# An attention and FFN kernel: RMS weight loaded first, GpSimd's order pinned, two more FFN tiles on the first token half

## The chip, the cores and the metric

The kernel runs on one core of one Trainium2 chip. The metric is device microseconds (us) of one execution, the median of several. The kernel before takes 265.59 us (median of 3, 265.25 to 265.94). Every execution also has a mean granted TensorE clock, as a share of full rate.

## The reference

Windowed attention with four sink tokens, then a SwiGLU FFN with an RMS norm in front. Cut to what matters:

```python
# q, k, v: (4, 8, 768, 64); keep = is_sink (first 4 keys) | (0 <= row - col < 128)
scores = np.where(keep, scale * q @ k^T, -1e9)
x = softmax(scores) @ v                # -> (3072, 512) tokens x channels
xn = x / sqrt(mean(x * x) + 1e-6) * rms_g
g = xn @ w_gate                        # 512 -> 1536
out = (g * sigmoid(g) * (xn @ w_val)) @ w_out
```

## The kernel before

The 3072 tokens are 24 blocks of 128. Four blocks form a group G of 512 tokens for the FFN. TensorE alternates pieces of attention ("slots") with pieces of the FFN ("parts"); the function `weave` decides the order. GpSimd issues the q, k, v and weight loads, one after the other; the sync engine (SP) issues the rest.

The order of GpSimd's loads in the opening, in program order (a scheduler may move a load where the order isn't pinned):

```python
load_q(0); load_k(0); load_q(1); load_k(1); load_v(0); load_v(1); load_w(0)
load_q(2); load_k(2); load_w(1); load_q(3); load_v(2); load_k(3); load_v(3)
load_w(2); load_w(3); load_q(4); load_w(4); load_k(4); load_w(5)   # w: 256 of 1536 columns, gate and val
load_v(4)
for g in range(GB + 1, 2 * GB):            # GB = 4
    load_q(g); load_k(g); load_v(g)
load_wo(0); load_wo(1)                     # output weights, 1.5 MB
for g in range(2 * GB, NB): ...            # blocks 8 to 23
```

The opening and the first group. The first two blocks are done alone; the gate and value products of group 0 then run on the first token half (blocks 0 and 1, 256 columns), for FFN tiles 0 to FA - 1, while blocks 2 and 3 are still in attention. The second half and the other tiles follow:

```python
unit_warm(6)                               # six idle matmuls, 2.74 us
... # blocks 0 and 1
nc.vector.tensor_copy(out=gb[:, 0:1], in_=QKT[0][:, 1, 0, 0:1])   # holds the next load back
load_gb()                                  # RMS weight, broadcast to 128 partitions, 256 KB, from SP
...
unit_x(1)                                  # transposes of the normed x of block 1
unit_t1(2, 1)                              # transposes of block 2's k
...
fa, fb = [], []
for ft in range(0, FA, 2):                 # FA = 8
    fa += parts_f(0, (ft, ft + 1), slice(0, GN // 2))     # [gate, val], first token half
    fb += parts_f(0, (ft, ft + 1), slice(GN // 2, GN))    # second token half
for ft in range(FA, FTN):                  # FTN = 12
    fb += parts_f(0, (ft,), slice(0, GN))
weave(fa, [..., [lambda: unit_x(2), ...], [lambda: unit_x(3)]], first=True)
slots = [[lambda: unit_t1(4, 1), lambda: unit_t1(5, 0)],          # block 5's q transposes
         [lambda: unit_s(4, 0), lambda: unit_t1(5, 1)],           # scores need block 5's q
         [lambda: unit_s(4, 1)], [lambda: unit_sink_scores(0, 4)], [lambda: unit_t(6)], []]
```

The softmax here doesn't subtract the row's maximum and nothing guards it: scores larger than these inputs give would overflow.

Of the kernel before, what the change touches and what calls it, by code (L numbers as in the profile page):

```python
# [9 lines left out]
ALU = mybir.AluOpType  # L10
ACT = mybir.ActivationFunctionType
FP32 = mybir.dt.float32
BF16 = mybir.dt.bfloat16
I32 = mybir.dt.int32

P = 128
# [12 lines left out]
def kernel(  # L29
# [13 lines left out]
    nc = tc.nc  # L43

    B, H, S, D = q.shape
    DM = H * D
    DFF = moe_w_gate.shape[1]
    NS = int(n_sink)
# [14 lines left out]
    NEG = -32768.0  # L63
# [2 lines left out]
    DMA_T_FROM = 12  # L66

    DMA_X_FROM = 8
    FA = 8
    WEAVE_FROM = 9  # L70
    POOL_MASK_FROM = 2
    MANUAL = {mybir.EngineType.PE, mybir.EngineType.SP}
# [8 lines left out]
    xpool = ctx.enter_context(tc.tile_pool(name="xpool", bufs=3))  # L81
# [17 lines left out]
    gb = const.tile([P, DM], FP32, name="gb")  # L99
# [16 lines left out]
    def load_q(g):  # L116
        QS[g] = load_block(q, "qs", g)

    def load_k(g):
        KS_[g] = load_block(k, "ks", g)  # L120

    def load_v(g):
        b, t = divmod(g, NT)
        nc.gpsimd.dma_start(
            out=V16[b][:, t, :, 0:D],
            in_=v[b, :, t * P:(t + 1) * P, :].rearrange("h t d -> t h d"),
        )
# [7 lines left out]
    def load_w(c):  # L135
        cols = slice(c * WCH, (c + 1) * WCH)
        nc.gpsimd.dma_start(out=wg[:, :, cols], in_=wg_src[:, :, cols])
        nc.gpsimd.dma_start(out=wv[:, :, cols], in_=wv_src[:, :, cols])

    def load_wo(c):  # L140
# [4 lines left out]
    ident = const.tile([P, P], BF16, name="ident")  # L145
# [4 lines left out]
    amasks = const.tile([P, 2, 2, P], BF16, name="amasks")  # L150
# [3 lines left out]
    sel = const.tile([P, P], BF16, name="sel")  # L154
    nc.vector.memset(sel, 0.0)
    headm = const.tile([P, H], BF16, name="headm")
    nc.vector.memset(headm, 1.0)

    load_q(0)
    load_k(0)  # L160
    nc.gpsimd.affine_select(
        out=ident, in_=ident, compare_op=ALU.not_equal, fill=1.0,
        base=0, pattern=[[-1, P]], channel_multiplier=1,
    )
    load_q(1)
    nc.gpsimd.affine_select(
        out=amasks[:, 1, 0, :], in_=amasks[:, 1, 0, :], compare_op=ALU.is_ge,
        fill=NEG, base=0, pattern=[[1, P]], channel_multiplier=-1,
    )
    nc.vector.tensor_scalar(  # L170
        out=amasks[:, 1, 1, :], in0=amasks[:, 1, 0, :], scalar1=-1.0, scalar2=NEG,
        op0=ALU.mult, op1=ALU.add,
    )
    nc.vector.tensor_copy(out=amasks[:, 0, :, :], in_=amasks[:, 1, :, :])
    nc.vector.memset(amasks[0:NS, 0, :, :], 0.0)
    load_k(1)
    load_v(0)
    load_v(1)
    load_w(0)
    load_q(2)  # L180
    load_k(2)
    load_w(1)
    load_q(3)
    load_v(2)
    load_k(3)
    load_v(3)
    nc.gpsimd.affine_select(
        out=sel[:, 0:H * NS].rearrange("p (h s) -> p h s", s=NS),
        in_=sel[:, 0:H * NS].rearrange("p (h s) -> p h s", s=NS),
        compare_op=ALU.not_equal, fill=1.0,  # L190
        base=0, pattern=[[0, H], [-1, NS]], channel_multiplier=1,
    )
    nc.gpsimd.affine_select(
        out=headm, in_=headm, compare_op=ALU.is_ge, fill=0.0,
        base=0, pattern=[[-NS, H]], channel_multiplier=1,
    )
    nc.gpsimd.affine_select(
        out=headm, in_=headm, compare_op=ALU.is_ge, fill=0.0,
        base=NS - 1, pattern=[[NS, H]], channel_multiplier=-1,
    )  # L200
    load_w(2)
    load_w(3)
    load_q(4)
    load_w(4)
    load_k(4)
    load_w(5)
    load_v(4)
    for g in range(GB + 1, 2 * GB):
        load_q(g)
# [19 lines left out]
    def unit_t1(g, i):  # L229

        b, t = divmod(g, NT)
        if t == 0 and i == 0:
            QKT[b] = qkt.tile([P, 2, HP, S], BF16, name="qkT")
        kind = dict(tag="ph", bufs=6) if PROLOGUE[0] and g == 2 else dict(tag="b1")
        ps = pp[0].tile([P, 512], FP32, name="pqk", **kind).bitcast(BF16)
        transposes(ps, (QS, KS_)[i].pop(g), 0)
        (nc.scalar.copy if g != 1 and i == 0 else nc.vector.tensor_copy)(  # L237
            out=QKT[b][:, i, :, t * P:(t + 1) * P],
            in_=ps[:, 0:HP * P].rearrange("p (x c) -> p x c", c=P),
        )  # L240

    def load_gb():
        nc.sync.dma_start(
            out=gb, in_=moe_rms_g.rearrange("(o d) -> o d", o=1).to_broadcast((P, DM)),
        )

    def by_dma(g):
# [222 lines left out]
    def unit_rms(g):  # L470
# [31 lines left out]
        if g >= 2:  # L502
            unit_xr(g)
# [3 lines left out]
    def unit_xr(g):  # L507
        y, x16 = Y.pop(g), X16.pop(g)
        XR[g] = []
        for c in halves(g):  # L510
            XR[g].append(xpool.tile([P, c.stop - c.start], BF16, name="xr", bufs=4))
            nc.vector.scalar_tensor_tensor(  # L512
                out=XR[g][-1], in0=x16[:, c], scalar=y[:, 4:5], in1=gb[:, c],
                op0=ALU.mult, op1=ALU.mult,
            )
        if g >= DMA_X_FROM:
            G, tb = divmod(g, GB)
            if tb == 0:
                XNT[G] = xtpool.tile([P, KTN, GN], BF16, name="xnt")
            nc.sync.dma_start_transpose(  # L520
                out=XNT[G][:, :, tb * P:(tb + 1) * P], in_=XR.pop(g)[0],
            )
# [120 lines left out]
    with tc.manual_schedule(engines=MANUAL_ALL):  # L643
        unit_warm(6)
        unit_t1(0, 0)
        unit_bias(0, 0)
        unit_t1(0, 1)
        unit_bias(0, 1)
        unit_sp(0, 0)
        unit_t1(1, 0)  # L650
        unit_bias(1, 0)
        nc.vector.tensor_copy(out=gb[:, 0:1], in_=QKT[0][:, 1, 0, 0:1])
        load_gb()
        unit_sp(0, 1)
        unit_t1(1, 1)
        unit_av(0, 0)
        unit_norm(0, 0, PV[(0, 0)])
        unit_sp(1, 0)
        unit_av(0, 1)
        unit_norm(0, 1, PV[(0, 1)])  # L660
        unit_sq(0, 0)
        unit_sq(0, 1)
        unit_warm(WARM[0])
        for u in range(2):
            unit_av(1, u)
            unit_norm(1, u, PV[(1, u)])
            unit_sq(1, u)
        unit_rms(0)
        unit_xr(0)
        unit_rms(1)  # L670
        unit_xr(1)
        unit_warm(WARM[1])
        unit_x(0)
        unit_t1(2, 0)
        unit_warm(WARM[2])
        unit_x(1)
        unit_t1(2, 1)
        nc.vector.tensor_scalar(
            out=masks, in0=amasks, scalar1=-1.0 / NEG, scalar2=1.0,
            op0=ALU.mult, op1=ALU.add,  # L680
        )
        pools.close()
        pp[0] = ctx.enter_context(
            tc.tile_pool(name="psum", bufs=4, space=bass.MemoryType.PSUM)
        )
        PROLOGUE[0] = False

    with tc.manual_schedule(engines=MANUAL):


        fa, fb = [], []
        for ft in range(0, FA, 2):
            fa += parts_f(0, (ft, ft + 1), slice(0, GN // 2))
            fb += parts_f(0, (ft, ft + 1), slice(GN // 2, GN))
        for ft in range(FA, FTN):
            fb += parts_f(0, (ft,), slice(0, GN))
        weave(fa, [
            [lambda: unit_bias(1, 1), lambda: unit_sp(1, 1), lambda: unit_sink(0)],
            [lambda: unit_t1(3, 0), lambda: unit_s(2, 0)],
            [lambda: unit_s(2, 1), lambda: unit_sink_scores(0, 2)],  # L700
            [lambda: unit_t1(3, 1), lambda: unit_bias(3, 0), lambda: unit_av(2, 0), lambda: unit_sp(3, 0), lambda: unit_av(2, 1)],
            [lambda: unit_av(3, 0)],
            [lambda: unit_av(3, 1), lambda: unit_t1(4, 0)],
            [lambda: unit_x(2), lambda: unit_bias(3, 1), lambda: unit_sp(3, 1)],
            [lambda: unit_x(3)],
        ], first=True)
        slots = [[lambda: unit_t1(4, 1), lambda: unit_t1(5, 0)], [lambda: unit_s(4, 0), lambda: unit_t1(5, 1)], [lambda: unit_s(4, 1)], [lambda: unit_sink_scores(0, 4)], [lambda: unit_t(6)], []]
        for g in range(5, NB + 3):
            slots += step(g)
        slots[6].pop()  # L710
        slots[10].pop()
        outs = []
        n = 0
        for G in range(NG):

            parts = fb if G == 0 else []
            for ft in range(FTN if G > 0 else 0):
                parts += parts_f(G, (ft,), slice(0, GN))
                if ft % 3 == 2 and outs:
                    parts += outs.pop(0)  # L720
            outs = [parts_o(G, tb) for tb in range(GB)]
            if G < WEAVE_FROM or G == NG - 1:
                for o in outs:
                    parts = parts + o
                outs = []
            n1 = 6 + 4 * ((G + 2) * GB + 2 - 5) + 1
            weave(parts, slots[n:n1], 1)
            n = n1
# [33 lines left out]
```

## Time and profile before

| | before |
|---|---|
| time | 265.59 us |
| span of the profiled execution | 263.1 us |
| TensorE busy | 94% |
| TensorE busy, first 50 us | 39.7 of 50 us |
| output products of group 0 begin | 61.71 us |

First the page: the line of busy times, and the slices (40 of 6.6 us each; a digit is tenths busy, or tenths of full clock granted). TensorE is full nearly everywhere but in the opening, and its clock drops in the third and fourth slice.

```profile
PE 246.1 (94%) x1746; PEld 123.6 (47%) x1746; DVE 179.9 (68%) x472; ACT 138.2 (53%) x277; POOL 98.2 (37%) x131
...
PE   5867979999999999999999998999999999999994
...
PEclk9988999999999999999999999999999999999999
```

The chain of work that ended last, followed back from the last instruction; columns are start, duration and what. Between 11 and 38.7 us it is a chain of loads, and its last link is block 5's q.

```profile
11.25 9.23 DMA wv<-in_moe_w_val_dram
...
21.15 8.07 DMA wv<-in_moe_w_val_dram
...
29.50 9.18 DMA qs<-in_q_dram
...
39.13 0.89 PE pg L552 x8
```

The timeline of TensorE: start, duration, what, and in brackets the idle time before it and what ended it. `pw` are idle warm-up matmuls, `pxt` the x transposes, `pqk` the q and k transposes, `pg` and `pvl` gate and value products, `pT` and `pss` the scores, `po` the output products.

```profile
12.46 1.89 PE L313 MATMUL pw<-idle 128*128 128x512 bf16 x8
16.90 0.40 PE L534 MATMUL pxt<-ident,xr 128*128 128x128 bf16 x4 [2.55 <-DVE xr L512]
...
17.36 2.00 PE L313 MATMUL pw<-idle 128*128 128x512 bf16 x5
...
35.38 0.40 PE L534 MATMUL pxt<-ident,xr 128*128 128x128 bf16 x4 [1.21 <-DVE xr L512]
...
38.73 0.40 PE L224 MATMUL pqk<-ident,qs 128*128 128x128 bf16 x4 [0.37 <-DMA qs<-in_q_dram]
38.96 1.04 PE L552 MATMUL pg<-xnt,wg 128*128 128x256 bf16 x8
39.93 0.39 PE L367 MATMUL pT<-qkT 64*128 64x256 bf16 x4
...
61.71 1.03 PE L593 MATMUL po<-wo,hT 128*128 128x512 bf16 x4
```

Five warm-up matmuls take 2.00 us after the 2.55 us gap, eight took 1.89 us before it. The record of the clock has half rate from 17.69 to 21.10 us. The 2.55 us gap is a wait for VectorE, and VectorE waited for the RMS weight (timeline of VectorE):

```profile
16.09 0.75 DVE L512 SCALAR_TENSOR_TENSOR xr<-x_342,y,gb 128x512 bf16<-128x512 bf16 x1 [1.52 <-DMA gb<-in_moe_rms_g_dram]
```

### The profile page before, as it was taken

The numbers are of one execution on the slowest core, as the hardware profiler recorded it, in microseconds if no ns is written. First come the engines' busy times: TensorE is split into PE (matmuls) and PEld (weight loads), VectorE is DVE, ScalarE is ACT, GpSimd is POOL, SyncE is SP. The second block draws the span as 40 slices with busy tenths as digits, with TensorE's granted clock in tenths as the row PEclk, the third lists the DMA queues.
The fourth block names the chain that finished last, engine by engine and source line by source line (L and its number), as shares of the span: only waits on it lengthen the run. The fifth ranks groups of instructions, "written<-read, shape, count | busy, mean of one in ns | idle before, by whom it ended". The sixth has DMA issues, their size and how long they took to land.

```text
span 263.1 us, 4755 instructions
## 1 busy us (share of the span) xinstructions
PE 246.1 (94%) x1746; PEld 123.6 (47%) x1746; DVE 179.9 (68%) x472; ACT 138.2 (53%) x277; POOL 98.2 (37%) x131
## 2 busy tenths in 40 slices
PE   5867979999999999999999998999999999999994
PEld 1435757645454444444454443444444454444441
DVE  3653786899768999438898449799338894078700
ACT  2635667687886546456455454465554532233211
POOL 8978679389989260413212001114212000000000
PEclk9988999999999999999999999999999999999999
DMA  9999999999999999452111450312330112200022
GB/s 58 138 176 178 186 169 174 197 156 151 169 178 174 146 143 147 95 159 42 22 21 40 97 165 20 62 20 41 102 101 1 22 20 60 107 16 0 0 80 80
DMA packets 105990, 25.73 MB, mean 98 GB/s; under 512 B 95088, under 2 KB 102768, under 8 KB 105968
## 3 DMA queue, kind: packets, MB, share of 16 engines
q0 software_dynamic: 82784, 14.16, 75.6%
q1 hardware_dynamic: 23184, 11.28, 18.6%
q8 instruction: 13, 0.21, 0.4%
q14 instruction: 9, 0.07, 0.1%
HBM read 28.57 MB, written 6.29 MB: 133 GB/s over the span
## 4 chain that ended last, share of the span: by engine, by line
PE 73%; DMA 10%; DVE 6%; ACT 4%; POOL 3%; issue 2%; ACTq 0%; POOLq 0%
PE pg L552 22%; PE po L593 21%; PE pvl L552 21%; DMA wv<-in_moe_w_val_dram 7%; PE pT L367 4%; DMA qs<-in_q_dram 3%; ACT et L374 2%; PE pv L427 1%; PE pv L423 1%; DVE et L387 1%; PE pqk L224 1%; PE pss L299 1%; PE pv L415 1%; DVE xr L512 1%; POOL qs L111 1%
## 5 line engine op out<-in xcount | busy, mean ns | idle before, releaser
L552 PE MATMUL pg<-xnt,wg 128*128 128x512 bf16 (+1 forms) x320 | 74.3, 359 | 2.3 <-DVE p_2576 L570 1.7
L552 PE MATMUL pvl<-xnt,wv 128*128 128x512 bf16 (+1 forms) x320 | 74.0, 358 | 0.2 <-ACT xnt L538 0.2
L593 PE MATMUL po<-wo,hT 128*128 128x512 bf16 x288 | 66.7, 379 | 0.0
L565 ACT ACTIVATE th<-pg 128x512 bf16<-128x512 f32 x72 | 42.8, 594 | 39.5 <-PE pg L552 39.1
L374 ACT ACTIVATE et<-pT 128x1024 bf16<-128x1024 f32 (+1 forms) x42 | 39.3, 936 | 10.4 <-PE pT L367 10.4
L389 POOL TENSOR_SCALAR_AFFINE_SELECT et<-et 128x512 bf16<-128x512 bf16 x20 | 12.7, 635 | 85.4 <-ACT et L374 79.6
L552 PEld LDWEIGHTS <-wg 128*128 128x128 bf16 x320 | 28.9, 98 | 29.6 <-issue 4.7
L552 PEld LDWEIGHTS <-wv 128*128 128x128 bf16 x320 | 29.6, 98 | 27.1 <-issue 1.3
L593 PEld LDWEIGHTS <-hT 128*128 128x128 bf16 x288 | 26.4, 98 | 29.5 <-issue 1.5
L600 ACT ACTIVATE osb<-po 128x512 f32<-128x512 f32 x24 | 14.3, 595 | 28.3 <-PE po L593 24.3
L111 POOL DMA_DIRECT2D qs<-in_q_dram x24 | 21.5, 897 | 7.1 <-DMA wo<-in_moe_w_out_dram 1.9
L111 POOL DMA_DIRECT2D ks<-in_k_dram x24 | 21.4, 890 | 6.5 <-DMA wo<-in_moe_w_out_dram 2.9
L450 DVE RECIPROCAL rden<-pv 128x4 f32<-128x4 f32 x48 | 8.5, 177 | 20.1 <-PE pv L427 20.0
L387 DVE TENSOR_TENSOR et<-et,masks 128x1024 bf16<-128x1024 bf16 (+1 forms) x22 | 14.1, 640 | 5.4 <-ACT et L374 5.3
L367 PE MATMUL pT<-qkT 64*128 64x256 bf16 (+1 forms) x168 | 15.6, 264 | 1.4 <-ACT qkT L237 0.7
L367 PEld LDWEIGHTS <-qkT 64*128 64x128 bf16 x168 | 5.1, 94 | 17.7 <-issue 17.5
L427 PEld LDWEIGHTS <-et 128*128 128x128 bf16 x168 | 11.6, 97 | 2.3 <-issue 0.7
L423 PEld LDWEIGHTS <-et 128*128 128x128 bf16 x136 | 10.8, 98 | 3.2
L394 POOL TENSOR_SCALAR_AFFINE_SELECT et<-et 128x512 bf16<-128x512 bf16 x16 | 11.0, 690 | 0.0
L415 PE MATMUL pv<-vsk,esk 128*128 128x260 bf16 x32 | 8.8, 274 | 0.0
L313 PE MATMUL pw<-idle 128*128 128x512 bf16 x22 | 7.4, 488 | 1.3 <-DVE idle L102 1.3
L264 ACT COPY qkT<-pqk 128x1024 bf16<-128x1024 bf16 x8 | 8.1, 1008 | 1.0 <-PE pqk L224 1.0
(319 smaller groups left out, 341.7 us busy)
## 6 DMA issues: line engine op xcount, KB each, us to landing
out_dram<-osb SPq DMA_DIRECT2D x24, 256.0 KB, 2.2
qs<-in_q_dram POOLq DMA_DIRECT2D x24, 128.0 KB, 8.2
ks<-in_k_dram POOLq DMA_DIRECT2D x24, 128.0 KB, 7.8
wg<-in_moe_w_gate_dram POOLq DMA_DIRECT2D x6, 256.0 KB, 8.5
wv<-in_moe_w_val_dram POOLq DMA_DIRECT2D x6, 256.0 KB, 8.7
wo<-in_moe_w_out_dram POOLq DMA_DIRECT2D x2, 768.0 KB, 10.5
v_100<-in_v_dram POOLq DMA_DIRECT2D x6, 128.0 KB, 8.3
v_102<-in_v_dram POOLq DMA_DIRECT2D x6, 128.0 KB, 7.7
```

Of the source, the lines that this page charges most:

```text
L111: nc.gpsimd.dma_start(out=tl, in_=src[b, :, t * P:(t + 1) * P, :].rearrange("h t d -> t h d"),)
L367: nc.tensor.matmul(out=pT[:, hi, j * 256:j * 256 + w], lhsT=QKT[b][pr, 1, hp, t * P:(t + 1) * P], rhs=QKT[b][pr, 0, hp, t * P:t * P + w], ...
L374: nc.scalar.activation(out=et[:, :, 0:nq, :].rearrange("p x n c -> p x (n c)"), in_=pT.rearrange("p i (j c) -> p (i j) c", c=256)[:, :, 0: ...
L387: nc.vector.tensor_tensor(out=ev, in0=ev, in1=mv, op=ALU.mult)
L389: nc.gpsimd.affine_select(out=et[:, :, 0, :], in_=et[:, :, 0, :], compare_op=ALU.is_ge, fill=0.0, base=0, pattern=[[0, 4], [1, P]], channe ...
L415: nc.tensor.matmul(out=pv[:, 0:HW], lhsT=ESK[(b, t)], rhs=VSK[b][:, 4 * u:4 * u + 4, :], start=True, stop=False, skip_group_check=True,)
L423: nc.tensor.matmul(out=dest, lhsT=E[(g - 1, h, 1)], rhs=V16[b][:, t - 1, h, :], start=(t == 1), stop=False, skip_group_check=True,)
L427: nc.tensor.matmul(out=dest, lhsT=E[(g, h, 0)], rhs=V16[b][:, t, h, :], start=(t == 0), stop=True, skip_group_check=True,)
L552: nc.tensor.matmul(out=ps[:, i * n:(i + 1) * n], lhsT=w_sb[:, kt, ft * P:(ft + 1) * P], rhs=XNT[G][:, kt, cols], start=(kt == 0), stop=(kt ...
L565: nc.scalar.activation(out=st["th"], in_=st["pg"], func=ACT.Tanh, scale=0.5)
L593: nc.tensor.matmul(out=st["po"], lhsT=HT[(G, ft // 2)][:, ft % 2, tb * P:(tb + 1) * P], rhs=wo[:, ft, :], start=(ft == 0), stop=(ft == FTN ...
L600: nc.scalar.mul(osb, st["po"], 0.5)
```

## The change

The intent: the RMS weight is there before it is needed; block 2's k transposes come behind the first gate product; and FFN tiles 8 and 9 also run on the first token half early, so that TensorE has work until blocks 2 and 3 join. (The change was described as also having one mask with a partial identity. The diff has no such thing.) Cut to its core:

```diff
-    FA = 8
+    FA = 10
...
+    nc.sync.dma_start(out=gb, in_=moe_rms_g...to_broadcast((P, DM)))
+    with tc.manual_schedule(engines={mybir.EngineType.Pool}):
         load_q(0)
         load_k(0)
         ...                       # same program order as before, now pinned
         load_w(5)
     load_v(4)                     # outside: the scheduler puts one v load ahead of load_w(2), at 15.87 us
...
-    xr ... bufs=4
+    xr ... bufs=3
...
-        nc.vector.tensor_copy(out=gb[:, 0:1], in_=QKT[0][:, 1, 0, 0:1])
-        load_gb()
...
-        unit_t1(2, 1)             # before the first gate part
...
-            [lambda: unit_bias(1, 1), lambda: unit_sp(1, 1), lambda: unit_sink(0)],
+            [lambda: unit_t1(2, 1), lambda: unit_bias(1, 1), lambda: unit_sp(1, 1), lambda: unit_sink(0)],
...
-            [lambda: unit_x(2), lambda: unit_bias(3, 1), lambda: unit_sp(3, 1)],
+            [lambda: unit_bias(3, 1), lambda: unit_sp(3, 1)],
+            [lambda: unit_x(2)],
+            [lambda: unit_t1(4, 1)],
             [lambda: unit_x(3)],
         ], first=True)
-        slots = [[lambda: unit_t1(4, 1), lambda: unit_t1(5, 0)], ...
+        slots = [[lambda: unit_t1(5, 0)], ...
```

More of the change, by code (lines that the diff above doesn't have):

```diff
@@ L157 @@
     nc.vector.memset(headm, 1.0)
-    load_q(0)
-    load_k(0)
-    nc.gpsimd.affine_select(
-        out=ident, in_=ident, compare_op=ALU.not_equal, fill=1.0,
-        base=0, pattern=[[-1, P]], channel_multiplier=1,
-    )
-    load_q(1)
-    nc.gpsimd.affine_select(
-        out=amasks[:, 1, 0, :], in_=amasks[:, 1, 0, :], compare_op=ALU.is_ge,
-        fill=NEG, base=0, pattern=[[1, P]], channel_multiplier=-1,
-    )
-    nc.vector.tensor_scalar(
-        out=amasks[:, 1, 1, :], in0=amasks[:, 1, 0, :], scalar1=-1.0, scalar2=NEG,
-        op0=ALU.mult, op1=ALU.add,
-    )
@@ L174 @@
-    nc.vector.tensor_copy(out=amasks[:, 0, :, :], in_=amasks[:, 1, :, :])
-    nc.vector.memset(amasks[0:NS, 0, :, :], 0.0)
-    load_k(1)
-    load_v(0)
-    load_v(1)
-    load_w(0)
-    load_q(2)
-    load_k(2)
-    load_w(1)
-    load_q(3)
-    load_v(2)
-    load_k(3)
-    load_v(3)
-    nc.gpsimd.affine_select(
-        out=sel[:, 0:H * NS].rearrange("p (h s) -> p h s", s=NS),
-        in_=sel[:, 0:H * NS].rearrange("p (h s) -> p h s", s=NS),
-        compare_op=ALU.not_equal, fill=1.0,
-        base=0, pattern=[[0, H], [-1, NS]], channel_multiplier=1,
-    )
@@ L193 @@
-    nc.gpsimd.affine_select(
-        out=headm, in_=headm, compare_op=ALU.is_ge, fill=0.0,
-        base=0, pattern=[[-NS, H]], channel_multiplier=1,
-    )
-    nc.gpsimd.affine_select(
-        out=headm, in_=headm, compare_op=ALU.is_ge, fill=0.0,
-        base=NS - 1, pattern=[[NS, H]], channel_multiplier=-1,
-    )
-    load_w(2)
-    load_w(3)
-    load_q(4)
-    load_w(4)
-    load_k(4)
-    load_w(5)
+    nc.sync.dma_start(
+        out=gb, in_=moe_rms_g.rearrange("(o d) -> o d", o=1).to_broadcast((P, DM)),
+    )
@@ new lines @@
+    with tc.manual_schedule(engines={mybir.EngineType.Pool}):
+        load_q(0)
+        load_k(0)
+        nc.gpsimd.affine_select(
+            out=ident, in_=ident, compare_op=ALU.not_equal, fill=1.0,
+            base=0, pattern=[[-1, P]], channel_multiplier=1,
+        )
+        load_q(1)
+        nc.gpsimd.affine_select(
+            out=amasks[:, 1, 0, :], in_=amasks[:, 1, 0, :], compare_op=ALU.is_ge,
+            fill=NEG, base=0, pattern=[[1, P]], channel_multiplier=-1,
+        )
+        nc.vector.tensor_scalar(
+            out=amasks[:, 1, 1, :], in0=amasks[:, 1, 0, :], scalar1=-1.0, scalar2=NEG,
+            op0=ALU.mult, op1=ALU.add,
+        )
+        nc.vector.tensor_copy(out=amasks[:, 0, :, :], in_=amasks[:, 1, :, :])
+        nc.vector.memset(amasks[0:NS, 0, :, :], 0.0)
+        load_k(1)
+        load_v(0)
+        load_v(1)
+        load_w(0)
+        load_q(2)
+        load_k(2)
+        load_w(1)
+        load_q(3)
+        load_v(2)
+        load_k(3)
+        load_v(3)
+        nc.gpsimd.affine_select(
+            out=sel[:, 0:H * NS].rearrange("p (h s) -> p h s", s=NS),
+            in_=sel[:, 0:H * NS].rearrange("p (h s) -> p h s", s=NS),
+            compare_op=ALU.not_equal, fill=1.0,
+            base=0, pattern=[[0, H], [-1, NS]], channel_multiplier=1,
+        )
+        nc.gpsimd.affine_select(
+            out=headm, in_=headm, compare_op=ALU.is_ge, fill=0.0,
+            base=0, pattern=[[-NS, H]], channel_multiplier=1,
+        )
+        nc.gpsimd.affine_select(
+            out=headm, in_=headm, compare_op=ALU.is_ge, fill=0.0,
+            base=NS - 1, pattern=[[NS, H]], channel_multiplier=-1,
+        )
+        load_w(2)
+        load_w(3)
+        load_q(4)
+        load_w(4)
+        load_k(4)
+        load_w(5)
@@ L239, in unit_t1 @@
             in_=ps[:, 0:HP * P].rearrange("p (x c) -> p x c", c=P),
-        )
-    def load_gb():
-        nc.sync.dma_start(
-            out=gb, in_=moe_rms_g.rearrange("(o d) -> o d", o=1).to_broadcast((P, DM)),
         )
@@ L510, in unit_xr @@
         for c in halves(g):
-            XR[g].append(xpool.tile([P, c.stop - c.start], BF16, name="xr", bufs=4))
+            XR[g].append(xpool.tile([P, c.stop - c.start], BF16, name="xr", bufs=3))
             nc.vector.scalar_tensor_tensor(
@@ L703 @@
             [lambda: unit_av(3, 1), lambda: unit_t1(4, 0)],
-            [lambda: unit_x(2), lambda: unit_bias(3, 1), lambda: unit_sp(3, 1)],
+            [lambda: unit_bias(3, 1), lambda: unit_sp(3, 1)],
+            [lambda: unit_x(2)],
+            [lambda: unit_t1(4, 1)],
             [lambda: unit_x(3)],
         ], first=True)
-        slots = [[lambda: unit_t1(4, 1), lambda: unit_t1(5, 0)], [lambda: unit_s(4, 0), lambda: unit_t1(5, 1)], [lambda: unit_s(4, 1)], [lambda: unit_sink_scores(0, 4)], [lambda: unit_t(6)], []]
+        slots = [[lambda: unit_t1(5, 0)], [lambda: unit_s(4, 0), lambda: unit_t1(5, 1)], [lambda: unit_s(4, 1)], [lambda: unit_sink_scores(0, 4)], [lambda: unit_t(6)], []]
         for g in range(5, NB + 3):
```

## The prediction

> **What bounds the kernel now.** TensorE is busy 94% of the 263.1 us span (page, part 1), and nearly without a gap from 60 us to the last matmuls (windows view). So the change is worth what it takes from the opening's idle time: 10.3 us in the first 50. Gaps in the TensorE timeline: 2.55 us before block 0's x transposes (16.90), 0.61 before the first gate group (20.82), 0.67 (24.85), 0.35 (29.52), 1.21 before block 2's x transposes (35.38), 0.21 before block 3's (37.74), 0.37 before block 5's q transposes (38.73). The first is the RMS weight: issued at 8.79, 7.2 us to landing; VectorE waited 1.52 us for it (xr, 16.09). The chain of waits runs through DMA: weight loads, then block 5's q, issued 29.50, 9.18 us on its way; only from 39.1 on it is mostly TensorE.
>
> **What the change does.**
> 1. Weight broadcast first on the sync queue: takes the 1.5 us wait away, and moves its 256 KB from the crowded stretch 12 to 16 us to one where the DMA engines only start. At the 170 to 180 GB/s moved there, I estimate later loads come about 1 us earlier. Block 0's q may lose 0.3 us to it.
> 2. Five warm-up matmuls take 2.00 us after the 2.55 us gap, eight took 1.89 before it. [...] the slow stretch in the trace (about 17.4 to 20.8) agrees. A 1 us gap should shorten it: up to 0.8 us.
> 3. Block 2's k transposes (0.40) move behind the first gate: the 0.61 gap goes.
> 4. Tiles 8 and 9 run their first token half early: two groups of eight 256-column matmuls, 0.87 us each by their starts, so 1.74 us of work moves ahead of block 5's wait and fills the 1.21 and 0.21 gaps. Sixteen more matmuls, but eight of 256 columns cost the same 0.87 as four of 512: no net work.
> 5. GpSimd's order is pinned; one v load comes before weight chunks 2 to 5, which costs them about the 1 us gained in step 1.
> 6. Three xr buffers for four: nothing. The diff changes no mask or identity.
>
> **The sum.** Gaps removed: 1.5 + 0.8 + 0.6 + 1.2 + 0.2 = 4.3 us. Not all counts: TensorE would reach block 5's q at about 36 us and wait there, I estimate 1.5 us. So the gain is the 1.74 us of work done before that landing, plus about 1 us by which it comes earlier: 2.7. VectorE (84 to 91% busy from 40 to 60 us) with slightly denser attention slots may take back 0.2. From 60 us on the same work is only shifted; the 1.7 us stall near 164 us stays.
>
> **Predicted: 263.1 us**, 8 in 10 between 261.2 and 265.0. Faster by over 2%: 0.07; within 2%: 0.92; slower: 0.01.
>
> **If right, the profile shows** block 0's xr near 14.6 us without a DMA wait; the first gate near 18.6; no gaps before block 2's and 3's x transposes; one new wait of 1 to 2 us for block 5's q, landing near 37.7; the chain through DMA until there; matmul busy time after 60 us equal.
>
> **What would make it wrong.** If block 5's q lands as late as before (GpSimd's issue not DMA-limited), the gain is 1.7; if 2 us earlier, nearly 4. If block 4's q or k, or weight chunk 4 (needed near 34 us), comes late, the wait appears earlier, without further loss unless it outlasts block 5's. If VectorE paces 40 to 60 us, the lead is given back there. If the broadcast delays block 0's q, everything starts later.

The 0.8 us is the author's estimate and fits the trace: 2.00 us for five warm-up matmuls less five eighths of 1.89 is 0.82. That the gap has to do with the slow stretch, and that a shorter one shortens it, was supposed: the trace before shows only the one behind the other.

## More of the kernel before

`weave` spreads the slots evenly over the parts:

```python
def weave(parts, slots, upto=0, first=False):
    n, i = len(parts) - upto, 0
    for s, f in enumerate(parts):
        if first: f()
        while i < len(slots) and i < (s + 1) * len(slots) / n:
            for u in slots[i]: u()
            i += 1
        if not first: f()
```

## The result and the profile after

The changed kernel takes 264.31 us (median of 4, 263.85 to 264.47), beside 265.54 us for the kernel before in the same rounds. The ratio is 0.995, with a 95% interval from 0.9931 to 0.9969. Ratios here are always the mean time of one kernel's runs over that of the other's of the same rounds, so not quite the ratio of the medians quoted. Executions over 1.5% slower than the fastest of the same kernel are left out of the means. The time lies in the predicted range, but the gain is 1.2 us where 2.5 was predicted (265.59 to 263.1).

The page of the changed kernel. The clock is now full in the third and fourth slice, and low in the seventh, which lies from 39 to 46 us:

```profile
PE 244.9 (93%) x1735; PEld 125.7 (48%) x1762; DVE 178.9 (68%) x471; ACT 137.9 (53%) x277; POOL 98.4 (37%) x131
...
PE   5878969989999999999999997999999999999994
...
PEclk9999997999999999999999999999999999999998
```

The timeline of VectorE: the RMS weight is there, and block 0's x is scaled at 14.20 us with no wait.

```profile
14.20 0.75 DVE L511 SCALAR_TENSOR_TENSOR xr<-x_344,y,gb 128x512 bf16<-128x512 bf16 x1
```

The chain of work that ended last still runs through the loads, to block 5's q, which lands at 36.92 in place of 38.68 us:

```profile
11.28 7.45 DMA wv<-in_moe_w_val_dram
...
19.02 7.95 DMA wg<-in_moe_w_gate_dram
27.26 9.66 DMA qs<-in_q_dram
37.40 0.59 ACT qkT L241
```

The timeline of TensorE (line numbers moved by a few):

```profile
15.01 0.40 PE L533 MATMUL pxt<-ident,xr 128*128 128x128 bf16 x4 [0.88 <-DVE xr L511]
...
15.46 1.24 PE L312 MATMUL pw<-idle 128*128 128x512 bf16 x5
...
35.19 0.40 PE L533 MATMUL pxt<-ident,xr 128*128 128x128 bf16 x4
36.97 0.40 PE L228 MATMUL pqk<-ident,qs 128*128 128x128 bf16 x4 [1.39 <-DMA qs<-in_q_dram]
38.04 0.39 PE L366 MATMUL pT<-qkT 64*128 64x256 bf16 x4 [0.67 <-ACT qkT L241]
38.37 0.40 PE L228 MATMUL pqk<-ident,ks 128*128 128x128 bf16 x4
38.60 1.69 PE L551 MATMUL pg<-xnt,wg 128*128 128x256 bf16 x8
40.22 0.61 PE L366 MATMUL pT<-qkT 64*128 64x256 bf16 x4
40.76 1.76 PE L551 MATMUL pvl<-xnt,wv 128*128 128x256 bf16 x8
42.35 0.60 PE L298 MATMUL pss<-qkT,ksk 128*128 128x256 bf16 x4
42.78 1.04 PE L551 MATMUL pg<-xnt,wg 128*128 128x256 bf16 x8
...
60.95 1.03 PE L592 MATMUL po<-wo,hT 128*128 128x512 bf16 x3
```

Read it from the top. The five warm-up matmuls take 1.24 us, so the half rate of the opening is gone. No gap is left before block 2's and 3's x transposes. TensorE is done at 35.58 (36.97 less the wait of 1.39) and waits for block 5's q, as predicted. Then come two things that were not predicted. The scores (`pT`) follow the q transposes at once and wait 0.67 us for ScalarE's copy of them; in the kernel before a gate product lay between. And the next gate and value products take 1.69 and 1.76 us where their like takes 1.04: the record of the clock has half rate from 38.83 to 42.24 us. The output products begin at 60.95 us, 0.76 us earlier than before, though block 5's q came 1.76 us earlier and 1.74 us of work had been done ahead of it.

### The profile page after: what moved, and what is told of

It reads as the page before. It is cut to its first block, busy times and chain, and to the rows that moved or that the text cites. A ratio compares the mean times of both kernels' runs of the same rounds, so it can differ in the third digit from the quotient of the medians.

```text
span 262.4 us, 4760 instructions
## 1 busy us (share of the span) xinstructions
PE 244.9 (93%) x1735; PEld 125.7 (48%) x1762; DVE 178.9 (68%) x471; ACT 137.9 (53%) x277; POOL 98.4 (37%) x131
## 4 chain that ended last, share of the span: by engine, by line
PE 76%; DMA 10%; ACT 4%; DVE 4%; POOL 3%; issue 2%; POOLq 0%; ACTq 0%
PE pg L551 22%; PE pvl L551 21%; PE po L592 21%; PE pT L366 4%; DMA qs<-in_q_dram 4%; DMA wg<-in_moe_w_gate_dram 3%; DMA wv<-in_moe_w_val_dram 3%; PE pv L426 2%; ACT et L373 1%; PE pv L422 1%; PE pqk L228 1%; PE pv L414 1%; PE pss L298 1%; POOL qs L111 1%; ACT sq L464 1%
## 5 line engine op out<-in xcount | busy, mean ns | idle before, releaser
L592 PE MATMUL po<-wo,hT 128*128 128x512 bf16 x278 | 65.7, 379 | 0.5
L551 PEld LDWEIGHTS <-wv 128*128 128x128 bf16 x328 | 30.5, 99 | 28.2 <-issue 2.3
L551 PEld LDWEIGHTS <-wg 128*128 128x128 bf16 x328 | 30.1, 98 | 28.6 <-issue 4.0
L228 PE MATMUL pqk<-ident,qs 128*128 128x128 bf16 x56 | 5.5, 221 | 2.8 <-DMA qs<-in_q_dram 2.8
```

The lines of the kernel that those rows point to most:

```text
L551: nc.tensor.matmul(out=ps[:, i * n:(i + 1) * n], lhsT=w_sb[:, kt, ft * P:(ft + 1) * P], rhs=XNT[G][:, kt, cols], start=(kt == 0), stop=(kt ...
L592: nc.tensor.matmul(out=st["po"], lhsT=HT[(G, ft // 2)][:, ft % 2, tb * P:(tb + 1) * P], rhs=wo[:, ft, :], start=(ft == 0), stop=(ft == FTN ...
```

## The experiments

Two theories were set against each other. **Theory A, the clock:** the new wait for block 5's q, with the ScalarE wait after it, leaves TensorE so idle (40% busy in the 3.41 us before 38.83) that its clock goes to half rate, and that stretch of 3.41 us eats most of the lead. **Theory B, pacing:** VectorE (62% busy from 40 to 50 us in the changed kernel, 96% from 50 to 60) and ScalarE (64 and 76%) pace that stretch, so that any lead of TensorE is lost there anyway. Twelve runs were made, of nine kernels (three of them ran twice), on three chips. All were correct. A kernel is compared through its ratio to the kernel before on the same chip.

| run | median us | ratio to before | executions with clock 0.994 or less |
|---|---|---|---|
| changed kernel, first result | 264.31 | 0.9950 | 4 of 4 |
| r1_after_again | 264.28 | 0.9945 | 6 of 6 |
| r2_after | 264.08 | 0.9928 | 4 of 6 |
| e1_fill | 262.85 | 0.9912 | 0 of 5 |
| r2_fill | 263.00 | 0.9897 | 0 of 6 |
| e2_q5_first | 262.34 | 0.9900 | 0 of 6 |
| e3_gb_only | 263.63 | 0.9943 | 1 of 6 |
| r2_gb_only | 263.63 | 0.9921 | 2 of 6 |
| e4_slot | 262.73 | 0.9909 | 1 of 6 |
| e5_no_gb | 265.06 | 0.9971 | 5 of 6 |
| e6_q5_slot | 262.37 | 0.9874 | 0 of 4 |
| e7_q5_slot_q8 | 261.88 | 0.9864 | 0 of 4 |
| e8_warm8 | 261.27 | 0.9835 | 0 of 5 |

First: e1_fill, e2_q5_first, e3_gb_only, e4_slot. Second: r1_after_again, e5_no_gb, e6_q5_slot, e7_q5_slot_q8. Third: r2_after, r2_fill, r2_gb_only, e8_warm8. (One half-rate stretch of 3.41 us in 262 us is a mean clock of about 0.9935, so the last column counts executions that had at least one. It doesn't say where the stretch lay: that only the profiled execution of each run shows. The half rate at the very start isn't in this mean: the profile of r2_after has 1.000, though full rate began only at 9.04 us and the six warm-up matmuls before it took 2.74 us, 0.46 each, where the eight of the kernel before, at 12.46 us, took 1.89, 0.24 each.)

### e1_fill: the wait filled with idle matmuls

```diff
-        ps = pp[0].tile([P, 512], FP32, name="pqk", **kind).bitcast(BF16)
+        raw = pp[0].tile([P, 512], FP32, name="pqk", **kind)
+        ps = raw.bitcast(BF16)
+        if (g, i) == (5, 0):
+            for _ in range(4):
+                nc.tensor.matmul(out=raw, lhsT=idle[:, 0:P], rhs=idle, start=True, stop=True)
         transposes(ps, (QS, KS_)[i].pop(g), 0)
```

> The changed kernel with four idle 512-column matmuls in front of block 5's q transposes, in the PSUM tile that these overwrite; no work of the kernel is moved. They can start when that tile's last reader is done (VectorE, 36.06 us in the changed kernel's trace) and end about when the q lands (36.9). Theory A (the clock): [...] the half-rate stretch from 38.83 to 42.24 us cost about 1.6 us; filled, the stretch is gone and the time falls by 1.3 to 1.7 us, to about 262.8 us, with the first matmuls of the output projection starting about 1.5 us earlier than 60.95. Theory B (VectorE and ScalarE pace the stretch from 40 to 60 us): the half rate goes too, but TensorE then waits more before 60 us, the output projection starts within 0.4 us of 60.95, and the time stays at 264.3.

262.85 us, and no execution with a half-rate stretch. TensorE's timeline shows the four idle matmuls and, after the same wait for ScalarE, the gate product at full rate; the 3.41 us from 36.97 us on are 80% busy:

```profile
36.56 1.02 PE L243 MATMUL pqk<-idle 128*128 128x512 bf16 x4
...
39.15 1.04 PE L557 MATMUL pg<-xnt,wg 128*128 128x256 bf16 x8
```

The filling adds work and moves nothing, and the time falls, as theory A has it. The output products began at 59.92, 1.03 us earlier than in the changed kernel and not 1.5: in this execution the full rate of the opening began only at 9.66 us in place of 4.70, and the first gate product at 18.74 in place of 17.70. This alone isn't yet proof; r2_fill repeats it beside the changed kernel.

### e2_q5_first: block 5's q and k before weight chunk 5

```diff
         load_k(4)
+        load_q(5)
+        load_k(5)
         load_w(5)
...
     for g in range(GB + 1, 2 * GB):
-        load_q(g)
-        load_k(g)
+        if g > 5:
+            load_q(g)
+            load_k(g)
         load_v(g)
```

> The changed kernel with block 5's q and k loads issued before weight chunk 5 (which is needed only near 53 us) in place of after it: block 5's q should land 2 to 2.6 us earlier, near 34.5 us, before TensorE is ready for it (about 35.4). Theory A: the 1.39 us wait and the half-rate stretch are both gone, the time falls by 2.5 to 3 us to about 261.5 us. Theory B: the wait is gone, but waits for VectorE and ScalarE grow between 38 and 60 us; the time falls by less than 1 us.

262.34 us. The gain is smaller than theory A expected (261.5 us), but larger than theory B allows (under 1 us). The wait for block 5's q and the half rate are gone. Part of the lead went into a wall that I hadn't seen, block 8's q and k, at 54 us in TensorE's timeline:

```profile
54.04 0.40 PE L231 MATMUL pqk<-ident,qs 128*128 128x128 bf16 x4 [1.73 <-DMA qs<-in_q_dram]
55.00 0.40 PE L231 MATMUL pqk<-ident,ks 128*128 128x128 bf16 x4 [0.56 <-DMA ks<-in_k_dram]
```

These loads stand behind the output weights in GpSimd's queue. In the kernel before TensorE came to them at 54.52 and had no wait. (The profiled execution was the slowest of the six, 263.90 us, so these waits may be longer than usual.)

### e3_gb_only and r2_gb_only: the early weight broadcast alone

```diff
+    nc.sync.dma_start(out=gb, in_=moe_rms_g...to_broadcast((P, DM)))
     load_q(0)
     load_k(0)
...                                # all else as in the kernel before
-        nc.vector.tensor_copy(out=gb[:, 0:1], in_=QKT[0][:, 1, 0, 0:1])
-        load_gb()
```

> The kernel before with one thing changed: the RMS weight broadcast issued first, and the copy that held it back removed. My prediction's step 1: block 0's xr starts near 14.3 us with no DMA wait, and block 5's q lands 1 to 1.8 us earlier than 38.7. The gaps before block 2's and 3's x transposes stay. If the part alone is worth what the landing moves, the time falls by 1.5 to 1.8 us, to about 263.9 us, a little more than the whole change gave; if the whole change's gain came from the reordering, it falls by under 0.7 us.

263.63 us, ratio 0.9943: as expected, this one part gives about what the whole change gives (0.9950 and 0.9945). Block 5's q landed at 37.8 us, 0.9 earlier than before (1 to 1.8 was expected), and TensorE waited 1.27 us for it. So the wait comes with the early broadcast alone; here a gate product stands right behind the transposes, and this execution had no half-rate stretch.

> The kernel before with only the early weight broadcast, once more, on the same chip as the changed kernel. If the reordering and the ten tiles gain nothing net because of the half-rate stretch that they bring, this run and the changed kernel are within 0.2% of each other, and the filled one is 0.3 to 0.5% below both.

Again 263.63 us, ratio 0.9921 beside 0.9928 for the changed kernel on the same chip. The other parts of the change give nothing net in the median. They do bring the half-rate stretch more often: it fell in 14 of the 16 executions of the changed kernel and in 3 of these 12. One of the three was profiled: TensorE waited 1.93 us for block 5's q there, and half rate followed from 39.04 to 42.45 us. In r2_gb_only the two executions with a stretch took 264.86 us in the mean and the four without it 263.43, a split of 1.43 us within one program. The filled kernel on this chip is at 0.9897, 0.24% under this run, a little less than the 0.3% expected.

### e4_slot: a gate product again between block 5's q transposes and the scores

```diff
-        slots = [[lambda: unit_t1(5, 0)], [lambda: unit_s(4, 0), ...], ..., [lambda: unit_t(6)], []]
+        slots = [[lambda: unit_t1(5, 0)], [], [lambda: unit_s(4, 0), ...], ..., [lambda: unit_t(6)]]
```

> The changed kernel with the empty slot of the second weave moved to second place, so that the first gate group of the second token half comes between block 5's q transposes and the scores that need their copy (as in the kernel before; in the changed kernel two slots fall before the first group, since 27 slots are spread over 25 groups). The 0.67 us wait for ScalarE at 38.04 us should go. Theory A: the time falls by 0.5 to 0.7 us, and [...] by 2 us with the half-rate stretch gone too. Theory B: no change beyond 0.2 us.

262.73 us. TensorE's timeline shows the gate product right behind the transposes; the wait for ScalarE is gone and, in 5 of 6 executions, the half rate too:

```profile
37.47 0.40 PE L228 MATMUL pqk<-ident,qs 128*128 128x128 bf16 x4 [1.09 <-DMA qs<-in_q_dram]
37.70 1.04 PE L551 MATMUL pg<-xnt,wg 128*128 128x256 bf16 x8
38.67 0.39 PE L366 MATMUL pT<-qkT 64*128 64x256 bf16 x4
```

The one execution with a clock of 0.993 took 263.74 us; the other five took 262.05 to 263.17. This was my own oversight made visible. With ten tiles in the first half, 27 slots go over 25 parts; the step is 1.08, so two slots fall before the first part.

### r1_after_again and r2_after: the changed kernel itself, execution by execution

No edit.

> The changed kernel itself, unaltered, on the chip of the other runs of this call, to see how often the half-rate stretch falls in it. Each execution's mean granted clock tells: about 0.993 with one half-rate stretch of 3.41 us, 0.997 or more without. Theory A: executions with a clock of 0.994 or less take about 264 to 264.5 us, any with 0.997 or more about 262.8. Theory B: the time does not go with the clock (all 263.8 to 264.5).

Six executions, all with a clock of 0.991 to 0.994, 263.33 to 264.80 us; only two of them lie in the 264 to 264.5 us that theory A gave. In the profiled one the half rate runs from 39.60 to 43.01 us, behind waits of 1.53 and 0.67 us. They could not be set against any without the stretch.

> The changed kernel once more, unaltered, to stand on one chip beside the filled one and the one with only the early weight broadcast. So far all ten of its executions have a mean granted clock of 0.990 to 0.994 (a half-rate stretch in each). Theory A: again, every execution, at about 0.995 of the kernel before.

"Every execution" failed, and that is the best evidence: on one chip, the same program ran with and without the stretch.

| clock | us |
|---|---|
| 0.991 to 0.994 | 264.93, 264.14, 264.38, 264.02 (mean 264.37) |
| 1.000 | 262.70, 262.90 (mean 262.80) |

The difference is 1.57 us, from two executions and four. One of the two fast ones was profiled; the four with a stretch were not, so that theirs lay at the same place is taken from the two profiles. Its TensorE timeline has the same two waits, shorter by 0.42 us in the first, and then a gate and a value product at full rate:

```profile
37.07 0.40 PE L228 MATMUL pqk<-ident,qs 128*128 128x128 bf16 x4 [0.97 <-DMA qs<-in_q_dram]
38.14 0.40 PE L366 MATMUL pT<-qkT 64*128 64x256 bf16 x4 [0.67 <-ACT qkT L241]
38.47 0.40 PE L228 MATMUL pqk<-ident,ks 128*128 128x128 bf16 x4
38.70 1.04 PE L551 MATMUL pg<-xnt,wg 128*128 128x256 bf16 x8
39.99 1.05 PE L551 MATMUL pvl<-xnt,wv 128*128 128x256 bf16 x8
40.88 0.60 PE L298 MATMUL pss<-qkT,ksk 128*128 128x256 bf16 x4
...
59.47 1.03 PE L592 MATMUL po<-wo,hT 128*128 128x512 bf16 x4
```

From the start of this gate product to that of `pss` it takes 2.18 us (38.70 to 40.88); in the first result's profile 3.75 us (38.60 to 42.35). So the two traces, too, put the cost of the stretch at 1.57 us.

Why this execution escaped is looked for in how busy TensorE was before. Five of the 14 profiles have a stretch of half rate before 255 us, and in each it lasts 3.41 us. From where the record of full rate begins to where that stretch begins are whole multiples of the same 3.41 us: 13.65 us in the kernel before (4.04 to 17.69, four times), 34.13 in the first result (4.70 to 38.83, ten), 30.72 in r1_after_again (8.88 to 39.60) and r2_gb_only (8.32 to 39.04, nine each), 6.82 in e5_no_gb (10.58 to 17.40, two). The beginning of full rate itself falls anywhere from 4.04 to 10.61 us in the 14. So I cut each trace into pieces of 3.41 us, counted from there. The lines give piece, length, TensorE busy (instructions), clock granted, DMA share and GB/s. Kernel before, the piece in front of its half-rate stretch and the stretch:

```profile
14.28:17.69 3.41, 0.86 (x11) 1.00 1.86 173
17.69:21.10 3.41, 2.80 (x15) 0.50 1.97 173
```

The changed kernel, first result:

```profile
35.41:38.83 3.42, 1.36 (x19) 1.00 2.42 155
38.83:42.24 3.41, 3.41 (x20) 0.50 2.33 161
```

The changed kernel, the profiled fast execution of r2_after:

```profile
36.35:39.76 3.41, 2.02 (x22) 1.00 2.43 155
39.76:43.17 3.41, 3.41 (x37) 1.00 2.08 172
```

In the first result the piece in front begins 0.17 us before the wait, and is 40% busy. In r2_after it begins 0.25 us into the wait and reaches further into the gate product behind it; it is 59% busy. Its wait for the q was also 0.42 us shorter, so where the piece lies and the length of the wait aren't separated. Over all 14 profiles, the five stretches of half rate before 255 us each followed a piece 25 to 44% busy; no piece of 51% or more was followed by one (those before the beginning of full rate and of the last matmuls left out; among these, a piece of e4_slot from 255.66 us, 44% busy, was not followed by half rate, so the line isn't sharp). This is a reading of these traces and no rule. The filled runs show that matmuls in the wait kept the stretch away (none in 11 executions); at which busy share the clock falls was not shown. I didn't set where the pieces lie in an experiment, and can't.

### r2_fill: the filled wait, on the same chip

The edit of e1_fill.

> The kernel with four idle matmuls in the wait for block 5's q once more, on the same chip as the changed kernel. Theory A: no execution under 0.997 of clock, and 0.3 to 0.5% (0.9 to 1.4 us) faster than the changed kernel here. Theory B: the two within 0.1% of each other.

263.00 us, no execution under 0.997, ratio 0.9897 against the changed kernel's 0.9928 on this chip: 0.31% or 0.8 us of the mean. (The mean of the changed kernel here has its two fast executions in it.) Against its four executions with the stretch the filled kernel is 1.37 us faster, and against the two without it, 0.2 us slower. So filling the wait brings the time to about that of the two lucky executions, and does little else. The interval of r2_fill is 0.9873 to 0.9920 and that of the changed kernel 0.9896 to 0.9960; they overlap, and the split by clock within one program is the firmer proof.

### e5_no_gb: the change without the early broadcast

```diff
-    nc.sync.dma_start(out=gb, ...)            # first
...
         unit_bias(1, 0)
+        nc.vector.tensor_copy(out=gb[:, 0:1], in_=QKT[0][:, 1, 0, 0:1])
+        load_gb()
```

> The changed kernel with the RMS weight's load put back where the kernel before has it, and nothing else changed: reordering, ten tiles and the pinned GpSimd order alone. Block 0's x transposes wait again until 16.9 us and block 5's q lands near 38.7, so TensorE, ready earlier by the 1.2 us gap it no longer has, waits for it about 1 us. The gain left is the 1.74 us of work done before that landing, less up to 1.7 us where a half-rate stretch follows: 263.6 us in executions without one, up to 265.2 with one. If the broadcast is what the change lives on, this run is within 0.5% of the kernel before.

265.06 us, ratio 0.9971, within 0.5% of the kernel before. The one execution without a stretch took 264.58 us where 263.6 was expected. The mechanism expected was not there in the profiled execution. TensorE waited 2.88 us for xr before block 0's x transposes (at 18.13 us), the half rate of the opening came back at 17.40, and TensorE came to block 5's q so late (39.79) that it didn't wait at all. The size fits, the path does not: without the broadcast the rest never gets far enough ahead to meet the q. This profile also had a late start of the full rate (10.58 us), so its opening is an unfavourable one.

### e6_q5_slot and e7_q5_slot_q8: both mends, and the second wall

e6 has the edits of e2 and e4. e7 adds:

```diff
+    load_q(2 * GB)
+    load_k(2 * GB)
     load_wo(0)
     load_wo(1)
     for g in range(2 * GB, NB):
-        load_q(g)
-        load_k(g)
+        if g > 2 * GB:
+            load_q(g)
+            load_k(g)
         load_v(g)
```

> The two mends at once: block 5's q and k loaded before weight chunk 5, and the empty slot in second place. If the loads of block 8, which stand behind the 1.5 MB of output weights in the queue, are now the next wall (the run with only the early q waited 1.73 and 0.56 us for block 8's q and k at 54 us), this gives no more than either mend alone: 262.3 us, with over 2 us of waits for block 8's q and k. If it is not a wall, 261.5 us.

> As the run with both mends, and block 8's q and k issued before the output weights (first needed near 59 us) in place of after them. If block 8's loads were the second wall, its wait at 54 us goes and the time falls a further 1 to 1.5 us, to about 261 us, with the output projection starting near 58.3 us. If VectorE and ScalarE pace this stretch, the time stays at 262.3.

e6: 262.37 us, as expected, with waits of 1.53 and 0.59 us before block 8's transposes (the profile puts the first down to a VectorE instruction, the second to k's load). e7: 261.88 us. The second wall is gone, but the gain over e6 is 0.5 us by the medians and 0.3 by the means, not 1 to 1.5; with four executions of each, whose ratios' intervals overlap (0.9851 to 0.9897 and 0.9839 to 0.9888), it isn't clear of noise. TensorE's timeline of e7 shows block 8's transposes without a wait, and the next wait, for ScalarE, soon after:

```profile
51.66 0.40 PE L234 MATMUL pqk<-ident,qs 128*128 128x128 bf16 x4
51.89 0.39 PE L234 MATMUL pqk<-ident,ks 128*128 128x128 bf16 x4
...
54.36 0.39 PE L372 MATMUL pT<-qkT 64*128 64x256 bf16 x4 [0.86 <-ACT qkT L269]
```

The output products began at 58.76, against 59.35 in e6. So a part of theory B is true: where block 8's loads aren't waited for, ScalarE ends the waits, 0.86 us here and 0.61 before a value product at 57.02. (The changed kernel's first profile, which has no wait for block 8, has the same 0.86 us at 56.78.) The opening's late full rate in the profiled e7 (9.48, against 4.42 in e6) cost it 0.55 us by the first gate product; I didn't separate that share.

### e8_warm8: eight warm-up matmuls at the start

```diff
-        unit_warm(6)
+        unit_warm(8)
```

> The fastest version so far (early q and k of block 5, empty slot in second place, block 8's q and k before the output weights; 261.88 us) with eight idle matmuls at the start for six. In the profiles so far full rate began between 4.0 and 4.7 us or between 8.9 and 10.6, never between, and the late ones lost about 0.9 us by the first gate group. Six matmuls at half rate end at 4.0 us and TensorE then waits until 5.0 to 5.4 for block 0's q; eight end near 4.9. [...] it now also starts between 5.4 and 7, and the median falls by up to 0.5 us, to about 261.5; if not, no change.

("It" in the last sentence is full rate.)

261.27 us (260.92 to 262.26), ratio 0.9835: the fastest version, 1.65% under the kernel before, where the changed kernel on the same chip is 0.7% under. In its profile full rate began at 5.36 us, a place where none of the others has it. That is one execution, and e7 ran on another chip, so that the two extra matmuls gave the 0.6 us between the two is likely and not shown.

## Why the prediction was right or wrong

The time was forecast as 263.1 us and came at 264.31, inside 261.2 to 265.0. The range did part of the work: the gain, 1.23 us, was about half of the 2.5 forecast. The mechanism of the opening was read rightly; in the sum one term was missing and one was too small. A third, the landing of block 5's q, moved more than forecast, which by luck hid a part of these.

- **Step 1, the broadcast: right.** xr started at 14.20 (14.6 predicted) without a wait. Block 5's q landed 1.2 to 1.8 us earlier in the three profiles of the changed kernel, and 0.9 and 1.1 with the broadcast alone; about 1 was predicted. Block 0's q transposes began at 5.43 for 4.83, a cost of 0.6 and not 0.3 us, but the score matmuls of block 0, at 7.26 for 7.38, were not late.
- **Step 2, the clock of the opening: right.** The five warm-up matmuls went from 2.00 to 1.24 us, and the first gate product came at 17.70 to 18.22 us in the three profiles, where 18.6 was predicted: at 17.70 with full rate from 4.70 us on, at 18.16 and 18.22 with full rate from 8.88 and 9.04. (So a late beginning came with about 0.5 us by there, which counts for changes of this size.) The 3.41 us in front of the old slow stretch were 25% busy, with the gap of 2.55 us among them.
- **Steps 3 and 4: right.** The gaps of 0.61, 1.21 and 0.21 us are gone (0.46 us for ScalarE's copy stands before the first gate product), and TensorE waits 1.39 us for block 5's q, 1 to 2 predicted.
- **Steps 5 and 6: right as far as seen.** No profile shows a wait for a weight, or one for an xr buffer. (The matmul busy time after 60 us, predicted equal, was 197.1 and 195.1 us; the second trace has 27 matmul records fewer there, so this is no sharp test.)
- **"The sum": this is where it failed.** The new wait was counted as time lost, and as harmless because the work had been moved ahead of it. The runs show that it can cost more than its length: in 14 of 16 executions the mean clock shows a half-rate stretch (two were profiled, and there it stands right behind this wait), in none of 11 with the wait filled; it cost 1.57 us by the split within r2_after. The prediction reckoned with a slow stretch behind the gap that the change removes, in step 2, and not behind the one that it makes.
- **"May take back 0.2": too small.** The two profiles without this stretch in the middle, the kernel before and the fast one of r2_after, give the sum. Block 5's transposes moved from 38.73 to 37.07, 1.66 us. With 1.74 us of work ahead, the output products should begin 3.4 us earlier. They moved from 61.71 to 59.47, 2.24 us. So 1.16 us was taken back. The waits of TensorE between these points account for 1.11 of it: 0.67 for ScalarE (two slots before the first part), 0.26 for block 8's k and 0.43 for ScalarE near 54 us are new, the wait for ScalarE near 58 us grew by 0.29, and one of 0.54 for VectorE near 59 us went.

With both in: 1.66 + 1.74 - 1.16 - 1.57 = 0.67 us, and the profiled spans differ by 0.7 (263.1 and 262.4). The median gain of 1.23 us is larger than that, since the executions scatter by about a microsecond and the kernel before often has a half-rate stretch too (19 of its 34 executions have a clock of 0.994 or less). In the executions without the stretch, the changed kernel took 262.8 us, 0.3 from the prediction.

Theory B falls as the main cause: filling the wait with idle matmuls, which relieves neither VectorE nor ScalarE, won back most of the loss. Still open is how often the stretch falls elsewhere: 4 of 4, 6 of 6 and 4 of 6 executions had it, and what sets where full rate begins at the start (4.04 to 10.61 us) was not found.

## What to carry to other kernels

A wait that a change creates is not only its length: look at what the record of the clock shows behind it. In five of these 14 profiles, half rate for 3.41 us followed 3.41 us in which TensorE was 25 to 44% busy, and in the changed kernel that stretch cost 1.57 us, behind a wait of 1.39. Where such a stretch shows, put work or idle matmuls into the wait (none of the 11 filled executions had the stretch), or fetch earlier what it waits for (none of the 6 of e2_q5_first had it). When work is moved ahead of a load, find the next load that the faster engine will run into; here two stood in line (1.39 us for block 5's q, then 1.73 and 0.56 for block 8's q and k in e2_q5_first), and each wait went when the load was issued before weights that were needed much later (the time gained by the second isn't clear of noise). Look at the granted clock of every execution before comparing medians that differ by less than one percent: r2_after is one program with 262.80 us at 1.000 and 264.37 at 0.991 to 0.994.
